# Moving three operand splits, holding a fourth weight tile, and two tables of numbers in a fused attention, MLP and MLP kernel

## The chip, the core and the metric

The kernel runs on one core of a Trainium2 chip. The metric is the device time of one execution in microseconds (us). TensorE (PE) does the matmuls, VectorE (DVE), ScalarE (ACT) and GpSimd (POOL) the elementwise work, SyncE (SP) issues most of the DMAs, and POOL issues those that add while they copy.

## The reference

Chunked attention with a few memory keys, then two dense MLPs over 3072 tokens; only the shapes and the two MLPs matter here.

```python
x = attention(q, k, v, mem_k, mem_v)         # (3072, 512) after the heads are joined
def moe(x, w_in, w_out):                     # w_in (512, 2048), w_out (2048, 512)
    h = x @ w_in
    g = max(h, 0) + log1p(exp(-abs(h)))
    return g @ w_out
def moe2(x, w_in, w_out, alpha):             # the same shapes
    h = x @ w_in
    g = max(h, 0) + alpha * min(h, 0)
    return g @ w_out
out = moe2(moe(x))
```

## The kernel before

**Products of split operands.** Each float32 operand of the MLPs is kept as a high part (a rounded copy) and a low part (the rest), and one product is three matmuls: high by high, high by low, low by high. `high` makes the first by an ACT cast, `low` the second by a DVE subtraction; `ready(n)` does both for one operand of the second MLP. The split tiles `g` have three rooms, so a split is made at most two or three operands ahead of its matmuls.

**First part: attention and the first MLP.** 96 steps, each a product into `ps_hh` and one into `ps_o` of 12 matmuls. Attention tiles, the conversion of both layers' weights from 64-bit words (`convert_a`, `convert_b` on DVE, tiles `word`) and sums of the second layer's weights (`wsum`, `wst` on POOL and ACT, written to `in_ops` and `out_ops` in DRAM) are set among the steps by a planner, the class `Plan`: each piece has an engine, a guessed duration and a due time, and the planner emits the piece that can start first, and of those the one due first. Its order is the order of the program on every engine, since the engines work in order. `when[i]` is the planned time of step `i`; line 806 sets the due times of the 32 conversions of the second layer.

**Second part: the second MLP.** Tokens go in three pairs of blocks of 512. Both matmuls of a pair use a seven-product scheme on two by two blocks (as Strassen's, in Winograd's form). In the first half of a pair, eight quads (`quad`, L553) each make seven products of six matmuls into four PSUM banks, combine them with the copies `c1`, `c5` (ACT, tiles `tc`) and the sums `u2` and `plus` (DVE), and apply the activation; `G[k, q]` (tiles `gb`) is the result. In the other half (`second`, L618) seven passes of eight units each (56 units of six matmuls) use `w_out` tiles of 1 MB, each for four units: tile `k` serves units `4k` to `4k + 3`. The operands of the first units, `G[1, 0]` to `G[1, 2]`, are made in the first quads, long before.

**DMAs of the second half.** `load_w_out` brings a tile. `SUMS` names after which unit POOL issues an in-place addition of 1 MB, `slots[k, half] += slots[e, half]`, which makes an operand of a later pass. `load_y` brings the first MLP's results for the next pair (tiles `yraw`, four loads for each `h`), `sum_y` and `split_y` (tiles `yt`, `xop`) prepare them on DVE and ACT; `prepare` says in which units. At the end `load_w_in` brings the next pair's first weights. SP issues its DMAs in one order, and a DMA that waits for a room holds those behind it. All large tiles (`w_out`, `w_in`, `xop`, `gb`) share sixteen rooms.

Of the kernel before, what the change touches and what calls it, by code (L numbers as in the profile page):

```python
# [44 lines left out]
NQ = NF // 2  # L45
# [89 lines left out]
def attention_mlp_mlp_kernel(ctx: ExitStack, tc, qk, v, w1, w2, consts, out):  # L135
# [363 lines left out]
    PASSES = ((S1, T1, 1), (A11, B11, 0), (S2, T2, 1), (S3, T3, 0), (S4, B22, 3), (A12, B21, 2), (A22, T4, 1))  # L499


    SUMS = {4: (0, 1, 3), 8: (1, 1, 3), 12: (0, 0, 1), 16: (1, 0, 1), 24: (0, 1, 2), 28: (1, 1, 2)}

    def load_w_out(n):

# [5 lines left out]
    def product(p, n, ka, kb, ps, first):  # L511
        w, x = w_in.pop((n, ka)), x_op[p, kb]
        k = 0
        for h in range(2):
            for a, c in ((0, 0), (0, 1), (1, 0)):
                pe.matmul(
                    ps, lhsT=w[:, a, h * P:(h + 1) * P], rhs=x[:, c, h, :],
                    start=first and k == 0, stop=k == 5, skip_group_check=not first,
                )
                k += 1  # L520
# [24 lines left out]
    def copy(ps, tag, bufs=1):  # L545
        t = tpool.tile([P, N2], F32, tag=tag, name="tc", bufs=bufs)
        act.copy(out=t, in_=ps)
        return t

    def plus(out, in0, in1, op=ALU.add):  # L550
        dve.tensor_tensor(out=out, in0=in0, in1=in1, op=op)

    def quad(p, q, between, ahead):  # L553


        n, f0, f1 = p * NQ + q, 2 * q, 2 * q + 1
        if q % 4 == 0:
            for k in range(4):
                room = (wpool if k else xpool).tile([P, 4, N2], F32, tag="w" if k else "x", name="gb")
                slots[k, q // 4] = room  # L560
                for e in range(4):
                    G[k, q + e] = room[:, e, :]
        banks = [("acc", ps_acc)] * 4 if q % 2 else [("pa", ps_a), ("h", ps_h)] * 2
        x1, x4, x3, x2 = (bank(space, tag) for tag, space in banks)
        product(p, n, A11, B11, x1, True)
        c1 = copy(x1, "tb")
        product(p, n, S1, T1, x4, True)
        c5 = copy(x4, "tl")
        product(p, n, S2, T2, x2, True)
        u2 = tpool.tile([P, N2], F32, tag="ta", name="u2", bufs=2)  # L570
        plus(u2, x2, c1)
        product(p, n, S3, T3, x3, True)
        plus(x3, x3, u2)
        plus(G[3, q], x3, c5)
        n3 = negative(G[3, q], f1)
        between()
        product(p, n, A12, B21, x1, False)
        n0 = halves_of(x1, G[0, q])
        product(p, n, S4, B22, x4, False)
        ahead()  # L580
        prelu(G[3, q], n3, G[3, q])
        plus(G[1, q], x4, u2)
        minus_prelu(n0, f0, G[0, q])
        n1 = negative(G[1, q], f0)
        product(p, n, A22, T4, x3, False)
        prelu(G[1, q], n1, G[1, q])
        dve.scalar_tensor_tensor(out=G[1, q], in0=G[1, q], scalar=-1.0, in1=G[0, q], op0=ALU.mult, op1=ALU.subtract)
        n2 = halves_of(x3, G[2, q])
        minus_prelu(n2, f1, G[2, q])
        if q < NQ - 2:  # L590
            load_w_in(n + 2)
        else:
            for k in range(3)[2 * q - 2 * NQ + 4:][:2]:
                load_w_out(14 * p + k)

    def turn(c, b, d):

# [15 lines left out]
    def ready(n):  # L613
        i, q = divmod(n, NQ)
        src = G[PASSES[i][2], q]
        g2[n] = low(src, high(src, n))

    def second(p, todo):  # L618

        ps_of, kept, c, later = {}, {}, {}, []  # L620
        spaces = {S1: (ps_acc, "acc"), A11: (ps_h, "h"), S2: (ps_a, "pa"), S3: (ps_acc, "acc"), S4: (ps_a, "pa"), A22: (ps_acc, "acc")}

        def temp(key, m, tag):
            kept[key, m] = tpool.tile([P, N2], F32, tag=tag, name="u2", bufs=1 if tag in ("tb", "tl") else 2)
            return kept[key, m]

        def result(d, b, m):
            if m == 0:
                c[d, b] = rpool.tile([P, 2, N2], F32, tag="raw", name="c")
            return c[d, b][:, m, :]  # L630

        def after(ka, ps):

            sub = ALU.subtract
            if ka == S1:
                return [lambda m=m: act.copy(out=temp("p5", m, ("tb", "tl")[m]), in_=ps[m]) for m in range(2)]
            if ka == A11:
                return [lambda m=m: act.copy(out=temp("p1", m, "word"), in_=ps[m]) for m in range(2)]
            if ka == S2:
                return [lambda m=m: plus(temp("u2", m, "ta"), ps[m], kept["p1", m], sub) for m in range(2)]  # L640
            if ka == S3:
                return ([lambda m=m: plus(temp("u3", m, "word"), ps[m], kept["u2", m]) for m in range(2)]
                        + [lambda m=m: plus(result(1, 1, m), kept["u3", m], kept["p5", m], sub) for m in range(2)]
                        + [lambda m=m: plus(kept["u2", m], kept["u2", m], kept["p5", m], sub) for m in range(2)])
            if ka == S4:
                return [lambda m=m: plus(result(0, 1, m), ps[m], kept["u2", m]) for m in range(2)]
            if ka == A12:
                return [lambda m=m: act.activation(out=result(0, 0, m), in_=ps[m], func=AF.Identity, scale=-1.0) for m in range(2)]
            return [lambda m=m: plus(result(1, 0, m), kept["u3", m], ps[m], sub) for m in range(2)]

        for n in range(7 * NQ):
            i, q = divmod(n, NQ)
            ka = PASSES[i][0]
            w = w_out[14 * p + n // 4][:, n % 4]
            if q == 0:
                ps = ps_of[ka] = [bank(*spaces[ka]) for _ in range(2)] if ka in spaces else ps_of[A11]
            g = g2.pop(n)
            for m in range(2):
                for k, (a, e) in enumerate(((0, 0), (0, 1), (1, 0))):
                    pe.matmul(  # L660
                        ps[m], lhsT=w[:, a, m * P:(m + 1) * P], rhs=g[:, e, :], start=ka in spaces and q == 0 and k == 0,
                        stop=q == NQ - 1 and k == 2, skip_group_check=ka not in spaces,
                    )
            if n % 4 == 3:
                w_out.pop(14 * p + n // 4)
                if n // 4 + 3 < 14:
                    load_w_out(14 * p + n // 4 + 3)
            if n in SUMS:
                half, k, e = SUMS[n]
                nc.gpsimd.dma_start(out=slots[k, half], in_=slots[e, half], accum_op=ALU.add)  # L670
            if 0 < n < 7 * NQ - 2:
                ready(n + 2)
            if q == NQ - 1:
                later = after(ka, ps)
                while i == 6 and later:
                    later.pop(0)()
            elif later:
                later.pop(0)()
            if q == 6 and i > 3:
                d, b = ((1, 1), (0, 1), (0, 0))[i - 4]  # L680
                turn(c.pop((d, b)), 2 * p + b, d)
            for piece in todo.get(n, ()):
                piece()
            if n == 7 * NQ - 8 or n == 7 * NQ - 4:
                load_w_in((p + 1) * NQ + (n == 7 * NQ - 4))
        return lambda: turn(c.pop((1, 0)), 2 * p, 1)

    def prepare(p):

        if p >= NPAIRS:  # L690
            return {}
        todo = {}
        for h in range(2):
            at = 2 + 25 * h
            todo[at] = [lambda h=h: load_y(p, h)]
            for k in range(3):
                todo[at + 7 + k] = [lambda h=h, k=k: sum_y(p, h, k)]
            for n, k in enumerate((B11, B21, B22, T1, T2, T3, T4)):
                todo[at + 10 + 2 * n] = [lambda h=h, k=k: split_y(p, h, k)]
            todo[at + 11] = [lambda h=h: sum_last(p, h)]  # L700
        return todo

    def pairs(between):
        for p in range(NPAIRS):
            for q in range(NQ):
                quad(p, q, between, (lambda: [ready(n) for n in range(3)]) if q == NQ - 1 else lambda: None)
                between = lambda: None
            between = second(p, prepare(p + 1))
        between()
# [9 lines left out]
    when = [ZERO + STEP * i for i in range(len(steps) + 1)]  # L719
# [83 lines left out]
    add(("raw2", 0), "", 5.0, 0, lambda: load_raw(1, halves[0]), [("raw", 2 * NF - 1)], ["raw"])  # L803
    for j in range(4 * NQ):
        q, e = divmod(j, 4)
        k, due = halves[j], when[20 + 60 * j // (4 * NQ)]
        add(("ca2", j), "DVE", 1.35, due, lambda j=j: convert_a(1, halves[j]), [("raw2", j)] + ([("cv2", j - 1)] if j else []), ["word"])
        add(("cv2", j), "DVE", 1.42, due, lambda j=j: convert_b(1, halves[j]), [("ca2", j)], [], ["raw"])
        if j + 1 < 4 * NQ:
# [124 lines left out]
```

## Time and profile before

| | us |
|---|---|
| median of three runs | 1166.56 (1164.11 to 1166.74) |
| the profiled execution, its own time | 1168.74 |
| its span, first to last instruction | 1166.9 |
| PE busy | 1119.8 (96%) |
| DVE busy | 734.2 (63%) |
| ACT busy | 573.9 (49%) |
| POOL busy | 183.1 (16%) |
| mean granted TensorE clock of the core | 0.982 |

A busy share says only how long an engine had an instruction. What the kernel loses stands in the gaps of PE, in what ended each gap, and in the stretches in which the granted clock is below 1.

### The profile page before, as it was taken

To read this page: it belongs to the slowest core of one execution; us is meant where nothing else is said; L and a number is where in the kernel's file an instruction comes from. 1 tells how busy PE (TensorE), PEld (TensorE's weight loads), DVE (VectorE), ACT (ScalarE), POOL (GpSimd) and SP (SyncE) were. 2 spreads that over 40 slices of the span, in tenths; PEclk is the share of its full clock that TensorE was granted. 3 is DMA by queue.
4 is the path that set the end of the run, shared out by engine and by line. 5 is a ranking of instruction groups with operands and counts; after the bars stand their busy time and mean duration, and the time that the engine had idled before them with its cause. 6 is when DMAs were issued, how large, how long until landed. Compare 5 with 4: busy or idle time off the path is not lost.

```text
span 1166.9 us, 15807 instructions
## 1 busy us (share of the span) xinstructions
PE 1119.8 (96%) x5760; PEld 924.2 (79%) x5760; DVE 734.2 (63%) x1486; ACT 573.9 (49%) x1068; POOL 183.1 (16%) x182
## 2 busy tenths in 40 slices
PE   6889999999999999999999999998999989999998
PEld 5767888877888888888888888787888778887776
DVE  5978878666656555665442266677566658566464
ACT  5854334455534544453343255654455546456433
POOL 0101222434333243333230000010000100000100
PEclk9988999999999999999999999999999999999999
DMA  8833564657645554554344074899356896647961
GB/s 307 268 98 120 159 150 144 170 181 209 204 140 190 178 174 129 192 165 158 129 142 162 3 286 163 274 225 400 117 228 222 238 293 257 220 165 288 304 164 67
DMA packets 76765, 224.12 MB, mean 192 GB/s; under 512 B 6160, under 2 KB 28688, under 8 KB 69008
## 3 DMA queue, kind: packets, MB, share of 16 engines
q1 hardware_dynamic: 71792, 200.05, 48.7%
q0 software_dynamic: 4896, 23.07, 10.4%
q8 instruction: 45, 0.74, 0.3%
q14 instruction: 32, 0.26, 0.1%
HBM read 158.08 MB, written 46.14 MB: 175 GB/s over the span
## 4 chain that ended last, share of the span: by engine, by line
PE 77%; DVE 7%; DMA 7%; issue 5%; ACT 2%; POOL 1%; SPq 0%; POOLq 0%; ACTq 0%; DVEq 0%
PE ps_q L61 35%; PE ps_o L61 18%; PE ps_hh L61 18%; DMA wout<-out_ops 3%; PE ps_s L61 3%; DVE word L61 2%; PE ps_x L61 2%; PE ps_t L61 1%; DMA in_ops<-wst 1%; DMA gb<-gb 1%; DVE g L61 1%; DVE gb L61 1%; DMA qk<-in_qk_dram 1%; ACT tp L61 1%; DVE s_sb L61 1%
## 5 line engine op out<-in xcount | busy, mean ns | idle before, releaser
L61 PE MATMUL ps_o<-g,wsplit 128*128 128x512 f32 x1152 | 283.0, 395 | 3.5 <-DVE g L61 2.7
L61 PE MATMUL ps_hh<-x,wsplit 128*128 128x512 f32 x1152 | 282.3, 396 | 2.3 <-DVE x L61 1.3
L61 PE MATMUL ps_q<-g,wout 128*128 128x512 f32 x1008 | 243.7, 401 | 15.8 <-DMA wout<-out_ops 6.5
L61 PEld LDWEIGHTS ps_hh<-x,wsplit 128*128 128x128 f32 x1152 | 216.8, 190 | 47.9 <-DVE x L61 2.0
L61 PEld LDWEIGHTS ps_o<-g,wsplit 128*128 128x128 f32 x1152 | 215.7, 189 | 49.3 <-DVE g L61 3.5
L61 PEld LDWEIGHTS ps_q<-g,wout 128*128 128x128 f32 x1008 | 193.1, 193 | 62.7 <-ACT g L61 9.1
L61 PE MATMUL ps_q<-xop,win 128*128 128x512 f32 x1008 | 229.7, 389 | 0.0
L61 PEld LDWEIGHTS ps_q<-xop,win 128*128 128x128 f32 x1008 | 189.0, 188 | 39.2
L61 DVE TENSOR_TENSOR g<-ta,g 128x512 fp32r<-128x512 f32 x96 | 76.1, 795 | 145.5 <-ACT g L61 145.4
L61 DVE TENSOR_TENSOR g<-gb,g 128x512 fp32r<-128x512 f32 x168 | 112.7, 688 | 84.3 <-ACT g L61 83.4
L61 ACT CAST g<-gb 128x512 fp32r<-128x512 f32 x168 | 100.3, 621 | 107.3 <-PE ps_q L61 80.2
L61 ACT ACTIVATE ta<-ps_hh 128x512 f32<-128x512 f32 x96 | 57.5, 599 | 188.9 <-PE ps_hh L61 186.5
L670 POOL DMA_DIRECT2D gb<-gb x18 | 15.7, 871 | 502.4 <-DVE g L61 476.9
L61 DVE SCALAR_TENSOR_TENSOR word<-raw,word 128x512 int32<-128x512 int32 x128 | 92.0, 719 | 3.8
L61 ACT ACTIVATE tp<-gb 128x512 f32<-128x512 f32 x48 | 30.4, 633 | 98.6 <-DVE gb L61 98.5
L219 POOL TENSOR_TENSOR wst<-wsum,wst 128x512 fp32r<-128x512 f32 x32 | 44.0, 1376 | 141.3 <-ACT wst L61 127.6
L61 PE MATMUL ps_s<-qk 128*128 128x96 f32 x384 | 55.7, 299 | 10.2 <-DMA qk<-in_qk_dram 6.9
L61 ACT CAST g<-ta 128x512 fp32r<-128x512 f32 x96 | 59.7, 622 | 10.1 <-PE ps_o L61 8.0
L61 PEld LDWEIGHTS ps_s<-qk 128*128 128x128 f32 x384 | 53.2, 212 | 13.8 <-DMA qk<-in_qk_dram 6.0
L61 DVE SCALAR_TENSOR_TENSOR gb<-gb,tp 128x512 f32<-128x512 f32 x48 | 33.2, 692 | 48.4 <-ACT tp L61 48.4
L61 DVE TENSOR_SCALAR word<-word 128x512 f32<-128x512 f32 (+1 forms) x128 | 58.7, 459 | 4.4
L61 ACT ACT_TABLE_LOAD x40 | 51.3, 1283 | 1.4 <-PEq L924 0.7
(67 smaller groups left out, 980.4 us busy)
## 6 DMA issues: line engine op xcount, KB each, us to landing
wout<-out_ops SPq DMA_DIRECT2D x42, 1024.0 KB, 10.3
raw<-in_w_dram SPq DMA_DIRECT2D x64, 512.0 KB, 3.7
win<-in_ops SPq DMA_DIRECT2D x24, 1024.0 KB, 8.0
qk<-in_qk_dram SPq DMA_DIRECT2D x24, 832.0 KB, 5.6
win<-in_ops SPq DMA_DIRECT2D x24, 768.0 KB, 7.5
gb<-gb POOLq DMA_DIRECT2D x18, 1024.0 KB, 12.0
out_ops<-wst SPq DMA_DIRECT2D x56, 256.0 KB, 3.0
in_ops<-wst SPq DMA_DIRECT2D x24, 512.0 KB, 3.4
```

The costliest lines, as they stand in the source:

```text
L61: i = getattr(self.engine, name)(*args, **kw)
L219: nc.gpsimd.tensor_tensor(out=t[:, 1, :n], in0=src, in1=t[:, 0, :n].bitcast(F32), op=ALU.subtract)
L670: nc.gpsimd.dma_start(out=slots[k, half], in_=slots[e, half], accum_op=ALU.add)
```

## The change

The three splits of a pair's first units, which stood together behind the last quad's product S4, are made one behind the copy `c1`, one behind `c5`, and one behind the sum into `G[3, q]`. The last two quads load four `w_out` tiles, not three, and the loop over the units loads the tile that is four ahead, not three. Four of the six entries of `SUMS` stand at other units. `prepare` starts one unit earlier. The conversions of the second layer's weights are due from step 24 on, over 64 steps, not from step 20 over 60.

```diff
-    SUMS = {4: (0, 1, 3), 8: (1, 1, 3), 12: (0, 0, 1), 16: (1, 0, 1), 24: (0, 1, 2), 28: (1, 1, 2)}
+    SUMS = {3: (0, 1, 3), 7: (1, 1, 3), 12: (0, 0, 1), 16: (1, 0, 1), 29: (0, 1, 2), 36: (1, 1, 2)}
...
         product(p, n, A11, B11, x1, True)
         c1 = copy(x1, "tb")
+        ahead(0)
         product(p, n, S1, T1, x4, True)
         c5 = copy(x4, "tl")
+        ahead(1)
...
         plus(G[3, q], x3, c5)
+        ahead(2)
         n3 = negative(G[3, q], f1)
...
         product(p, n, S4, B22, x4, False)
-        ahead()
...
-            for k in range(3)[2 * q - 2 * NQ + 4:][:2]:
-                load_w_out(14 * p + k)
+            for k in range(2):
+                load_w_out(14 * p + 2 * (q - NQ + 2) + k)
...
-                if n // 4 + 3 < 14:
-                    load_w_out(14 * p + n // 4 + 3)
+                if n // 4 + 4 < 14:
+                    load_w_out(14 * p + n // 4 + 4)
...
-            at = 2 + 25 * h
+            at = 1 + 25 * h
...
-                quad(p, q, between, (lambda: [ready(n) for n in range(3)]) if q == NQ - 1 else lambda: None)
+                quad(p, q, between, ready if q == NQ - 1 else lambda n: None)
...
-        k, due = halves[j], when[20 + 60 * j // (4 * NQ)]
+        k, due = halves[j], when[24 + 64 * j // (4 * NQ)]
```

What stands on the engines, by the built programs:

ACT in the last quad of the first pair, from its copies on. `tc` are `c1` and `c5`, the casts to `g` are the high parts, `tp` and `gb` are the activation's steps. Before:

```order
L61 COPY tc<-ps_q 128x512 x2
L61 ACTIVATE tp<-gb 128x512
L61 ACTIVATE tp<-tp,cst 128x512
L61 ACTIVATE tp<-ps_q 128x512
L61 ACTIVATE gb<-ps_q 128x512
L61 CAST g<-gb 128x512 x3
```

After:

```order
L61 COPY tc<-ps_q 128x512
L61 CAST g<-gb 128x512
L61 COPY tc<-ps_q 128x512
L61 CAST g<-gb 128x512 x2
L61 ACTIVATE tp<-gb 128x512
L61 ACTIVATE tp<-tp,cst 128x512
L61 ACTIVATE tp<-ps_q 128x512
L61 ACTIVATE gb<-ps_q 128x512
```

The three casts moved ahead of the four activations that they followed. DVE in the same quad; the rows `g<-gb,g` are the low parts. Before:

```order
L61 TENSOR_TENSOR u_6350<-ps_q,tc 128x512
L61 TENSOR_TENSOR ps_q<-ps_q,u_6350 128x512
L61 TENSOR_TENSOR gb<-ps_q,tc 128x512
L61 TENSOR_TENSOR g<-gb,g 128x512 x3
L61 SCALAR_TENSOR_TENSOR gb<-gb,tp 128x512
L61 TENSOR_TENSOR gb<-ps_q,u_6350 128x512
```

After:

```order
L61 TENSOR_TENSOR g<-gb,g 128x512 x2
L61 TENSOR_TENSOR u_6356<-ps_q,tc 128x512
L61 TENSOR_TENSOR ps_q<-ps_q,u_6356 128x512
L61 TENSOR_TENSOR gb<-ps_q,tc 128x512
L61 TENSOR_TENSOR g<-gb,g 128x512
L61 SCALAR_TENSOR_TENSOR gb<-gb,tp 128x512
L61 TENSOR_TENSOR gb<-ps_q,u_6356 128x512
```

Two of the three subtractions moved ahead of `u2`, the third stayed behind the sum into `G[3, q]`. SP in the first pair (the second pair reads alike), from the end of its quads to the loads for the next pair. Before:

```order
L494 DMA win<-in_ops 128x2x768
L509 DMA wout<-out_ops 128x2048 x7
L460 DMA yraw<-y_dram 128x512
L509 DMA wout<-out_ops 128x2048
L460 DMA yraw<-y_dram 128x512 x3
L509 DMA wout<-out_ops 128x2048 x6
L494 DMA win<-in_ops 128x2x1024
```

After:

```order
L494 DMA win<-in_ops 128x2x768
L509 DMA wout<-out_ops 128x2048 x8
L460 DMA yraw<-y_dram 128x512 x2
L509 DMA wout<-out_ops 128x2048
L460 DMA yraw<-y_dram 128x512
L509 DMA wout<-out_ops 128x2048
L460 DMA yraw<-y_dram 128x512
L509 DMA wout<-out_ops 128x2048 x4
```

The eighth tile (number 7) moved ahead of all four `yraw` loads, number 8 ahead of two of them and number 9 ahead of one. In the third pair, which has no `yraw` loads, SP reads as before. POOL's rows, its six additions of each pair among them, stand in the order of before.

## Rows read from the trace of the kernel before

**Rows 1.** Waits of PE: who was waited for, us in total, times, longest.

```profile
PE ps_q L61 <- DMA wout<-out_ops: 6.5, 2, 3.5
PE ps_q L61 <- ACT g L61: 6.2, 7, 1.3
PE ps_q L61 <- DVE g L61: 3.1, 7, 0.7
...
PE ps_s L61 <- ACT pt L61: 2.4, 3, 1.5
```

**Rows 2.** PE's timeline, second part: start, us, matmuls, idle ahead and its end.

```profile
670.34 70.88 PE L61 MATMUL ps_q<-xop,win 128*128 128x512 f32 x312
...
748.95 39.49 PE L61 MATMUL ps_q<-g,wout 128*128 128x512 f32 x173 [0.74 <-DVE g L61]
791.94 11.14 PE L61 MATMUL ps_q<-g,wout 128*128 128x512 f32 x42 [3.50 <-DMA wout<-out_ops]
...
913.93 41.10 PE L61 MATMUL ps_q<-g,wout 128*128 128x512 f32 x173 [0.74 <-DVE g L61]
```

**Rows 3.** Stretches: length, busy PE, PEld, DVE, ACT, POOL, clock, DMA share, GB/s.

```profile
200.00:660.00 460.00, 454.62 (x2557) 377.30 (x2557) 258.26 (x594) 206.37 (x339) 138.79 (x136) 1.00 0.51 162
236.00:244.00 8.00, 7.43 (x60) 6.63 (x61) 5.33 (x23) 2.47 (x7) 2.09 (x2) 0.79 0.61 174
792.00:796.00 4.00, 4.00 (x12) 3.20 (x13) 0.00 (x0) 0.00 (x0) 0.00 (x0) 0.65 1.02 430
914.00:918.00 4.00, 4.00 (x11) 3.13 (x12) 1.77 (x3) 0.62 (x1) 0.87 (x1) 0.57 0.66 133
958.00:964.00 6.00, 5.98 (x19) 4.77 (x20) 0.91 (x3) 0.62 (x1) 0.00 (x0) 0.72 1.01 427
1080.00:1086.00 6.00, 5.76 (x18) 4.59 (x19) 3.18 (x6) 1.76 (x3) 0.97 (x2) 0.72 1.02 374
```

**Rows 4.** ACT's timeline in the first pair's last quad.

```profile
734.24 1.08 ACT L61 COPY tc<-ps_q 128x512 f32<-128x512 f32 x2
...
739.37 0.72 ACT L61 ACTIVATE tp<-tp,cst 128x512 f32<-128x512 f32 x1
...
740.95 1.66 ACT L61 CAST g<-gb 128x512 fp32r<-128x512 f32 x3
```

**Rows 5.** DVE's timeline in the same quad and behind it.

```profile
735.88 0.69 DVE L61 TENSOR_TENSOR u<-ps_q,tc 128x512 f32<-128x512 f32 x1 [0.39 <-PE ps_q L61]
737.17 0.70 DVE L61 TENSOR_TENSOR ps_q<-ps_q,u 128x512 f32<-128x512 f32 x1 [0.60 <-PE ps_q L61]
...
741.60 1.90 DVE L61 TENSOR_TENSOR g<-gb,g 128x512 fp32r<-128x512 f32 x3 [2.93 <-ACT g L61]
743.42 0.68 DVE L61 SCALAR_TENSOR_TENSOR gb<-gb,tp 128x512 f32<-128x512 f32 x1
...
748.21 1.89 DVE L61 TENSOR_TENSOR g<-gb,g 128x512 fp32r<-128x512 f32 x3
```

**Rows 6.** SP's timeline of DMA issues, first pair.

```profile
722.21 18.00 SPq L509 DMA_DIRECT2D wout<-out_ops  x7
...
766.39 1.15 SPq L509 DMA_DIRECT2D wout<-out_ops  x1
769.10 5.36 SPq L460 DMA_DIRECT2D yraw<-y_dram  x3
774.55 14.24 SPq L509 DMA_DIRECT2D wout<-out_ops  x5
```

**Rows 7.** The DMA issued at 774.5: count, KB, us from issue to landing.

```profile
wout<-out_ops SPq DMA_DIRECT2D x1, 1024.0 KB, 17.3
```

**Rows 8.** The stretch of the six additions, columns as in rows 3.

```profile
750.00:788.00 38.00, 38.00 (x169) 31.49 (x168) 26.19 (x42) 22.00 (x39) 4.44 (x6) 1.00 1.01 221
```

**Rows 9.** POOL's timeline, first pair: the fifth of the six additions.

```profile
769.97 0.87 POOL L670 DMA_DIRECT2D gb<-gb  x1 [4.82 <-DVE g L61]
```

**Rows 10.** The chain that ended last, third pair, ahead of unit 28.

```profile
1101.15 15.33 DMA gb<-gb
```

## Prediction

> **What bounds the kernel now.** I began with the busy shares (PE 96%) and then asked what ends PE's gaps. The view of waits [rows 1] gives three causes in the second part: w_out tiles that have not landed (6.5 us, twice), and high and low parts of operands `g` (6.2 and 3.1 us, seven times each). PE's timeline [rows 2] says where. The eight quads run without a gap, 312 matmuls in 70.88 us, so a matmul has a slot of 0.227 us; then the first four units of the other half stutter, and at 791.94 PE waits for a tile. The view by stretches [rows 3] adds what no wait shows: behind such a gap the granted clock mostly falls, for some us, to its lower level (1.2 of 2.4 GHz). So the kernel is bound by PE, with losses at a few places:
>
> - Start of the units. From 670.34 to the second matmul of unit 3, at 748.95, lie 331 matmuls [rows 2], 75.2 us at 0.227; it took 78.6. The loss is 3.4 us, and the first part of rows 1's waits repeats it in each of three pairs. In the second pair the clock then stands at 0.57 for 4 us, in the third at 0.72 for 6 [rows 3]: 0.43 x 4 = 1.7 and 0.28 x 6 = 1.7 us. In the first pair it does not fall (1.00 from 750 on [rows 8]).
> - Tile 8. The 173 matmuls from 748.95 would end at 788.25; unit 32 starts at 791.94, 3.7 us late, and the clock takes 0.35 x 4 = 1.4 us more. The second pair has 3.0 (what is left of 6.5), 3.2 by position, and 1.7 of clock at 958.
> - Unit 28 of the third pair, behind an addition that took 15.33 us [rows 10].
> - First part, 200 to 660 us: 460 - 454.6 = 5.4 us of idle PE, and 0.21 x 8 = 1.7 us of clock at 236 [rows 3]: with the fill of the pipeline some 8 us.
>
> **The splits (moved).** Before, three casts (740.95, 1.66 us) and three subtractions (741.60, 1.90 us) stand on ACT and DVE in the middle of the last quad's activation [rows 4, 5]. ACT had finished what DVE's step at 743.42 needs by 740.09 (739.37 + 0.72): that step, and the whole chain to the low part of unit 3 (the first of three at 748.21), waits 3.3 us for the subtractions. In the new order the first two splits go into the idle time ahead. That isn't quite free: ACT has two copies from 734.24 (1.08 us) and now two casts with them (1.1), so the second high part is there at 736.4, its subtraction ends at 737.0, and `u2` starts there, not at 735.9. Behind it the sum at 737.17 had 0.6 us of slack on PE, so it becomes 0.7 later (the third subtraction then runs while ACT works). DVE's step thus starts at 740.8, 2.6 us earlier, and so does the chain to unit 3: its low part is there at 746.3. PE, with units 0 to 2 ready at once, wants it at 670.34 + 75.2 = 745.5. **2.65 us of the 3.4 are gained, 0.8 stay.** A gap of that size cost no clock where I see one (the first pair's larger one didn't), so the 1.7 us in pairs two and three go too.
>
> **Tiles and y loads (moved).** The first seven tiles leave SP from 722 on, in one burst [rows 6]: a tile goes as soon as a room is free, not at the unit where the code has it. Tile 7 then stands behind the first `yraw` load (766.39), and tile 8 behind the next three, which wait for rooms that DVE's work on `xop` gives back; it is issued only at 774.55 and takes 17.3 us [rows 6, 7]. What it waits for otherwise is tile 2's room, free since unit 11, near 761. In the new order tile 7 is in the burst, and tile 8 goes behind the second `yraw`, at 769.10 before; `prepare`, one unit earlier, takes 1.4 us off that and the start of the units 2.65. So it is issued near 765, and unit 32 wants it at 746.3 + 39.3 = 785.6. With its 17.3 us it lands at 782. That price lies high: tile 7's place in the queue is gone from ahead of it, though two loads and the additions still share the engines.
>
> A limit remains. From 750 on the DMA engines are full (share 1.01 over 38 us [rows 8]), so until 791.8 they moved what they could: six additions, four `yraw`, tiles 7 and 8. With tile 7 in the burst, tile 9 takes its place in that sum, and lands between 789 and 792.5; unit 36 wants it 24 matmuls after unit 32, at 791.0. I leave 0.7 us in each pair for it (bounds 0 and 1.5, and 1.4 more if the clock falls). Behind unit 23 the order of tiles is as before.
>
> First pair: 2.65 + 3.7 + 1.4 - 0.7 = 7.0 us. Second pair: 2.65 + 1.7 + 3.2 + 1.7 - 0.7 = 8.5 us.
>
> **The third pair.** It has no `yraw` loads, and its SP order is unchanged. Unit 28 waits for the fourth addition, which waits for the second, and that for the low part of unit 7; an addition takes 15 us there [rows 10]. This chain starts with the first operands, 2.65 us earlier. What PE gains beyond, the 1.7 us of clock, it waits at unit 28, and the clock falls there as before. Gain 2.65 us (bounds 1 and 8, worked out below).
>
> **`SUMS` (four entries moved).** Nothing. The fifth addition stands behind unit 24 in the code, yet POOL issued it at 769.97, when PE was 92 matmuls past 748.95, in unit 18; it had waited for a subtraction of DVE [rows 9]. POOL does little else in the second part, its order is unchanged, and its additions wait for the operands read before, which are the same ones. Units 29 and 36 don't hold it back either.
>
> **Due times of the conversions.** They start four steps later, when the first layer's conversions are nearly done, and lie a little further apart; the last ends some five steps later, under 80 to 86 of 96, where PE has no gap. The order of DVE, ACT, POOL and SP in the first part changes throughout, so each of the old gaps can go and new ones come. Bounds: all 8 us gained; two places like that at 236 (1.5 us of waiting [rows 1] and 1.7 of clock) lost, 6.4 us. I take 2 us of gain, nearer to nothing.
>
> **Sum.** 7.0 + 8.5 + 2.65 + 2 = 20.2 us. The profiled execution took 1168.7 us (span 1166.9), so 1148.5; the runs' median is 2.2 us below the profile, so 1146.4 for a median. I say 1147.
>
> **Rivals.**
> A. *The full DMA engines stay the bound in pairs one and two.* All that changes for tile 8 is then that tile 7 (2.4 us at the 430 GB/s of the stretch at 792 [rows 3]) is out of the way: it lands at 791.8 - 2.4 = 789.4, PE waits 3.8 us at unit 32, and the clock falls as before. Pair one gains 2.5 us, pair two some 3.3 to 4, with the rest 10.5 to 11: 1156. For it: share 1.01 [rows 8], and 17.3 us for 1 MB. Against: within those 41.8 us tile 8 was issued late, so two additions got ahead of it that now run beside it. [...]
> B. *The third pair's additions are not the bound.* The second one is issued some 4 us earlier (2.65, and unit 7 lay behind the slow clock). If the chain keeps up, unit 28's wait (the last of the seven in rows 1's first two kinds, 1.5 us, about 2 by position) and the clock's fall behind it, 1.7 as elsewhere, go as well as the 1.7 ahead: 8 us for the pair, and with a better first part 1141. Against: tiles and additions share the engines there, and starting additions earlier puts them beside more of the tiles.
> C. *Slower: the first part's new order.* ACT takes its casts of `wst` in order, and one that waits for a staging room holds attention's copies behind it; at 236 that cost 1.5 + 1.7 us. Seven such places more than before would outweigh 20 us and make the kernel slower by the bound. For it: conversions now run through to the last attention tiles. Against: they are less dense, and the whole stretch has five us of gaps today.
> D. *The splits move and nothing follows*, because unit 0 waits for a PSUM bank: it needs the one that the activation of A12's product empties, just ahead of the casts at 740.95 before [rows 4] and 0.7 us later after; only the unit's second half uses it, three matmuls after the start at 741.2, so this costs 0.1 us at most. Little speaks for it.
>
> **How the numbers follow.** Forecast 0.58 (1143 to 1151), A 0.2 (1152 to 1158), B 0.1 (1138 to 1143), a first part that loses 3 to 6 us with the rest as forecast 0.07 (1150 to 1156), C 0.04, D 0.01. The range 1139 to 1157 leaves out about 0.15. What a measurement can tell from no change is 0.3%, 3.5 us: 1163 and 1170. Faster 0.93; same 0.04 (A with a loss in the first part); slower 0.03.
>
> **What would show it.** Right: PE's gaps at the start of the units shrink to one below 1 us at unit 3, with no fall of the clock behind it; tile 8 leaves SP some 7 us earlier against PE's progress and the wait for w_out in units 32 to 36 is below 1.5 us a pair; the third pair still waits at unit 28, longer than before; POOL's additions keep their places between PE's units. Wrong: a w_out wait of 3 us or more (A), new waits of PE of more than 8 us in all between 200 and 660 (C), a chain on DVE that is late by more than 0.7 us at `u2`, or a gap between units 33 and 46, where DVE has a subtraction, a combination and y work in nearly every unit and no time to spare.

## The result and the profile after

The changed kernel took 1146.57 us (median of four runs, 1145.29 to 1147.35) against 1165.96 us of before in the same runs: a ratio of 0.9835, 95% interval 0.9818 to 0.9852. It is faster by 1.65%, 19.4 us; the prediction was 1147. The profiled execution took 1145.29 us, its span is 1143.4.

PE's waits in the second part, where [rows 1] had three kinds; w_out is gone from the list:

```profile
PE ps_q L61 <- ACT g L61: 3.1, 3, 2.2
PE ps_q L61 <- DVE g L61: 2.7, 7, 0.6
```

PE's timeline of the second part, answering [rows 2] (start, us, matmuls, idle ahead and what ended it; the rows left out have at most 0.23 us of idle time ahead of them):

```profile
665.12 70.88 PE L61 MATMUL ps_q<-xop,win 128*128 128x512 f32 x312
...
741.05 49.05 PE L61 MATMUL ps_q<-g,wout 128*128 128x512 f32 x215 [0.63 <-DVE g L61]
...
803.32 0.51 PE L61 MATMUL ps_q<-g,wout 128*128 128x512 f32 x1 [0.18 <-ACT g L61]
...
823.33 70.98 PE L61 MATMUL ps_q<-xop,win 128*128 128x512 f32 x312
...
899.37 49.09 PE L61 MATMUL ps_q<-g,wout 128*128 128x512 f32 x215 [0.59 <-DVE g L61]
...
962.28 0.50 PE L61 MATMUL ps_q<-g,wout 128*128 128x512 f32 x1 [0.74 <-ACT g L61]
...
982.29 70.98 PE L61 MATMUL ps_q<-xop,win 128*128 128x512 f32 x312
...
1058.32 29.06 PE L61 MATMUL ps_q<-g,wout 128*128 128x512 f32 x126 [0.63 <-DVE g L61]
1087.60 5.55 PE L61 MATMUL ps_q<-g,wout 128*128 128x512 f32 x23 [0.23 <-DVE g L61]
1095.38 0.50 PE L61 MATMUL ps_q<-g,wout 128*128 128x512 f32 x1 [2.22 <-ACT g L61]
1096.10 15.07 PE L61 MATMUL ps_q<-g,wout 128*128 128x512 f32 x65 [0.23 <-DVE g L61]
```

From 741.05 on, and from 899.37 on in the second pair, 215 matmuls run without a gap, where before they broke at unit 32. Two gaps are left in the first two pairs: below 1 us at unit 3, and one at unit 47 that the kernel before did not have. The third pair waits at units 24 and 28. Stretches, columns as in [rows 3], and the stretch of [rows 8]:

```profile
200.00:660.00 460.00, 458.50 (x2589) 381.33 (x2588) 258.70 (x599) 208.24 (x343) 139.11 (x136) 1.00 0.51 162
750.00:788.00 38.00, 38.00 (x169) 31.46 (x168) 29.17 (x47) 21.70 (x39) 3.48 (x4) 1.00 1.02 279
1095.00:1103.00 8.00, 7.40 (x31) 5.88 (x32) 4.53 (x8) 4.27 (x8) 0.87 (x1) 1.00 1.02 281
```

The first part's idle time fell from 5.4 to 1.5 us. The DMA engines are as full as before. Behind the longest gap the clock stays at 1.00. SP in the first pair, answering [rows 6]:

```profile
716.99 18.48 SPq L509 DMA_DIRECT2D wout<-out_ops  x8
756.74 2.28 SPq L460 DMA_DIRECT2D yraw<-y_dram  x2
759.11 1.19 SPq L509 DMA_DIRECT2D wout<-out_ops  x1
762.57 0.32 SPq L460 DMA_DIRECT2D yraw<-y_dram  x1
762.99 1.42 SPq L509 DMA_DIRECT2D wout<-out_ops  x1
```

POOL's fifth addition, answering [rows 9], 96.7 us behind the first quad's start (99.6 before):

```profile
761.84 0.87 POOL L672 DMA_DIRECT2D gb<-gb  x1 [4.19 <-DVE g L61]
```

DVE in the last quad, answering [rows 5]; two subtractions stand ahead of `u2` now, and the step into `G[3, q]` at 735.51 no longer waits for three:

```profile
731.17 0.69 DVE L61 TENSOR_TENSOR g<-gb,g 128x512 fp32r<-128x512 f32 x1 [0.29 <-ACT g L61]
731.78 0.68 DVE L61 TENSOR_TENSOR u<-ps_q,tc 128x512 f32<-128x512 f32 x1
...
735.51 0.69 DVE L61 SCALAR_TENSOR_TENSOR gb<-gb,tp 128x512 f32<-128x512 f32 x1 [0.92 <-ACT tp L61]
...
740.32 1.89 DVE L61 TENSOR_TENSOR g<-gb,g 128x512 fp32r<-128x512 f32 x3
```

The chain that ended last, ahead of unit 28 of the third pair, answering [rows 10]:

```profile
1079.17 15.43 DMA gb<-gb
```

**Where the time went.** The starts of the three quad stretches and of the last seven transposes (1137.76 after, 1161.20 before) cut an execution into four pieces. One execution is a weak witness, since the order of instructions doesn't change from run to run but the falls of the clock do. The profiled executions of the kernels below are used too, each for the pieces in which its order is that of before or that of the change. Means, with range and number of executions:

| piece | order of before | order of the change | gained | forecast |
|---|---|---|---|---|
| first part, to the first quad | 670.1 (668.7 to 672.2; 4) | 665.0 (661.8 to 666.5; 10) | 5.2 | 2 |
| first pair | 165.6 (164.9 to 166.6; 3) | 158.6 (158.2 to 158.8; 4) | 7.0 | 7.0 |
| second pair | 165.5 (164.4 to 166.3; 3) | 158.9 (158.5 to 159.3; 4) | 6.6 | 8.5 |
| third pair | 158.8 (157.5 to 160.0; 4) | 156.5 (155.5 to 157.4; 6) | 2.3 | 2.65 |

Their sum, 21.1 us from few executions, stands beside 19.4 by the medians.

### The profile page after: what moved, and what is told of

Read it like the earlier page. It is cut to its first block, busy times and chain, and to the rows that moved or that the text cites. A ratio compares the mean times of both kernels' runs of the same rounds, so it can differ in the third digit from the quotient of the medians.

```text
span 1143.4 us, 15784 instructions
## 1 busy us (share of the span) xinstructions
PE 1110.9 (97%) x5760; PEld 919.2 (80%) x5760; DVE 732.1 (64%) x1486; ACT 573.4 (50%) x1068; POOL 183.5 (16%) x182
## 3 DMA queue, kind: packets, MB, share of 16 engines
q0 software_dynamic: 4896, 23.07, 10.5%
## 4 chain that ended last, share of the span: by engine, by line
PE 83%; DMA 6%; DVE 5%; ACT 3%; POOL 1%; issue 1%; SPq 0%; ACTq 0%; DVEq 0%; POOLq 0%
PE ps_q L61 33%; PE ps_o L61 21%; PE ps_hh L61 21%; PE ps_s L61 3%; PE ps_x L61 2%; PE ps_t L61 2%; DMA out_dram<-o_sb 2%; DVE gb L61 2%; ACT tp L61 1%; DMA gb<-gb 1%; DMA in_ops<-wst 1%; DMA qk<-in_qk_dram 1%; DMA out_ops<-wst 1%; DVE g L61 1%; POOL wst L219 1%
## 5 line engine op out<-in xcount | busy, mean ns | idle before, releaser
L61 PE MATMUL ps_q<-g,wout 128*128 128x512 f32 x1008 | 235.2, 392 | 6.0 <-ACT g L61 3.1
L61 PEld LDWEIGHTS ps_q<-g,wout 128*128 128x128 f32 x1008 | 187.7, 188 | 49.8 <-DVE g L61 6.3
L61 DVE TENSOR_SCALAR word<-word 128x512 f32<-128x512 f32 (+1 forms) x128 | 62.9, 491 | 4.4
L219 POOL TENSOR_TENSOR wst<-word,wst 128x512 fp32r<-128x512 f32 (+1 forms) x32 | 36.6, 1144 | 118.4 <-ACT wst L61 118.4
```

The source lines that it names most:

```text
L61: i = getattr(self.engine, name)(*args, **kw)
L219: nc.gpsimd.tensor_tensor(out=t[:, 1, :n], in0=src, in1=t[:, 0, :n].bitcast(F32), op=ALU.subtract)
```

## The experiments

Ratios are to the kernel before, run beside each kernel on the same chip, with the 95% interval. A difference in us that stands behind a ratio is worked out from the ratio; a difference of two medians can lie up to 1.5 us off it.

**The splits alone.** The kernel before, with only this:

```diff
         c1 = copy(x1, "tb")
+        ahead(0)
...
         c5 = copy(x4, "tl")
+        ahead(1)
...
         plus(G[3, q], x3, c5)
+        ahead(2)
...
-        ahead()
```

> The kernel before, with the splits of units 0 to 2 moved and nothing else. Theory (the units' start and tile 8 are separate losses, and tile 8 is late because of its place in SP's queue): each pair gains the 2.65 us at unit 3, pair two 1.7 us of clock behind it, and the third pair what it gained in the whole change, 4.2 us; tile 8's wait stays as it was: about 2.65 + 4.35 + 4.2 = 11 us less than before, at least 8. Rival (the full DMA engines bound unit 32): what PE gains at unit 3 of pairs one and two it waits for at tile 8 instead, w_out waits of 9 us there in place of 6.5 to 7 in all, and only the third pair's 2.65 to 4.2 us are left: 3 to 5 us less than before.

Measured: 1157.79 us, 0.9925 (0.9903 to 0.9947), 8.7 us less. Unit 3's gap shrank as in the whole change. But the two waits for tile 8 grew, to 4.31 and 3.54 us, from 6.5 in all [rows 1] to 7.9. Tile 8 in the first pair, its issue, who waited for it, and its time to land:

```profile
L509 SPq DMA_DIRECT2D wout<-out_ops x1: 665/665/665, 770.3 to 770.3; - x1
...
  PE ps_q L61: 4.3, 1
...
DMA to landing us min/median/max: 18.1/18.1/18.1
```

It left 2.6 us earlier against the first quad (101.6 us behind it, 104.2 before) and landed 1.8 us earlier (119.7 and 121.5). Against the means of before the pairs are 1.3, 3.1 and 1.9 us shorter, and the first part 1.4. The size is at the lower end of the theory's (at least 8), and the pieces of this one execution add up to 7.7; in the first pair the rival's mechanism is at work.

**Tiles and y work alone.** The kernel before with `k + 4` tiles held and `at = 1 + 25 * h`.

> The kernel before, with four w_out tiles held and the y work one unit earlier; splits, additions and due times as before. Theory (order of issue): tile 8 leaves SP some 8 us earlier, its wait and the clock's fall behind it go in pairs one and two (3.7 + 1.4 and 3.2 + 1.7 us), the 3.4 us at the start of the units stay in all three: 10 us less than before, no wait for w_out above 1 us. Rival (full DMA engines): only tile 7's 2.4 us are saved in each of the two pairs, and the clock still falls: about 5 us less, with w_out waits of 1.3 and 0.8 us left.

Measured: 1157.42 us, 0.9931 (0.9915 to 0.9947), 8 us less, and no wait for w_out. Pairs one and two took 160.9 and 161.6 us, 4.7 and 3.8 less than the means of before. That lies between theory and rival in time, but the rival's left-over waits aren't there.

**Four tiles, and the y work's unit.** Two kernels take one of these back from the changed kernel. Three tiles held:

```diff
-                if n // 4 + 4 < 14:
-                    load_w_out(14 * p + n // 4 + 4)
+                if n // 4 + 3 < 14:
+                    load_w_out(14 * p + n // 4 + 3)
```

> The changed kernel with three w_out tiles held, as before; all else of the change kept. SP then sends tile 7 where the changed kernel sends tile 8, and tile 8 where it sends tile 9 (762.99 there, 20.7 us to its landing at 783.7; unit 32 wants it at 780.4). Theory (place in the queue decides): unit 32 waits 1 to 3.3 us in pairs one and two and the clock may fall behind it, 1.5 more: 3 to 8 us more than the changed kernel. Rival (the y work's earlier unit did it alone, the fourth tile nothing): within 1 us of the changed kernel.

The y work at its old unit (`at = 2 + 25 * h`):

> The changed kernel with the y work at its unit of before; all else of the change kept. SP then has one y load ahead of tile 8 and three more ahead of tile 9. Theory: tile 8 lands in time; tile 9 leaves some 101.5 us behind the first quad's start, as tile 8 did where the splits alone were moved, takes 18 to 20.7 us and is wanted 120.7 us behind that start: waits of 0 to 1.5 us in pairs one and two, 1.5 of clock with each at most: 0 to 6 us more than the changed kernel. Rival (four tiles did it alone): within 1 us of the changed kernel.

Measured: three tiles 1152.26 us, 0.9876 (0.9853 to 0.9899), 4 to 6 us slower than the change, as the theory had it. The old unit 1144.94 us, 0.9814 (0.9792 to 0.9837): not slower than the change, as the rival had it, with no difference clear of the noise; its first two pairs took 158.9 and 159.0 us, against means of 158.6 and 158.9 in the change. PE's timeline with three tiles, at unit 32:

```profile
783.97 11.17 PE L61 MATMUL ps_q<-g,wout 128*128 128x512 f32 x42 [3.44 <-DMA wout<-out_ops]
```

Tile 8 of that kernel, issue and landing:

```profile
L509 SPq DMA_DIRECT2D wout<-out_ops x1: 1040/1040/1040, 763.0 to 763.0; - x1
...
DMA to landing us min/median/max: 20.9/20.9/20.9
```

Tile 9 of the changed kernel, in the same place of SP's queue:

```profile
L509 SPq DMA_DIRECT2D wout<-out_ops x1: 1421/1421/1421, 763.0 to 763.0; - x1
...
DMA to landing us min/median/max: 20.7/20.7/20.7
```

The second tile behind the burst, by issue and landing in us behind the first quad's start:

| kernel | which tile | issued | landed |
|---|---|---|---|
| before | 8 | 104.2 | 121.5 |
| splits alone | 8 | 101.6 | 119.7 |
| change, old y unit | 9 | 101.6 | 119.4 |
| change, three tiles | 8 | 97.9 | 118.8 |
| change | 9 | 97.9 | 118.6 |

Leaving 6.3 us earlier brings 2.9 us, of which 1.8 came with the splits alone, which start the additions earlier as well. Between the change and the change with the old unit, where only the y work differs, 3.7 us bring 0.8. The place in time hardly counts, since the engines are full; what counts is that with a tile more in the burst the tile that lands at 119 is number 9, which unit 36 wants at 120.7, and not number 8, which unit 32 wants at 115.2 (741.05 - 665.12, 173 matmuls of 0.227 on, and 24 more).

**Due times alone.** The kernel before with `when[24 + 64 * j // (4 * NQ)]`.

> The kernel before, with the new due times of the conversions alone. Theory: no other part of the change reaches the first part, so this gives all of what the first part gained with the change, 5.2 us up to the first quad, of which 6.4 us lie behind 100 us and 1.2 us are lost ahead of it; pairs as before. Rival: the first part's gain needs nothing of the order but came from this execution's clock at the start (0.87 to 0.88 in the first 100 us); then this kernel gains below 2 us, as I forecast.

Measured: 1160.96 us, 0.9962 (0.9948 to 0.9976), 4.4 us less; the first quad starts at 666.50. PE's gaps in the first part behind 200 us, all four:

```profile
220.94 2.02 PE L61 MATMUL ps_s<-qk 128*128 128x96 f32 x16 [0.58 <-DVE x L61]
232.30 1.13 PE L61 MATMUL ps_s<-qk 128*128 128x96 f32 x8 [0.23 <-ACT pt L61]
...
627.12 0.50 PE L61 MATMUL ps_o<-g,wsplit 128*128 128x512 f32 x1 [0.27 <-ACT g L61]
628.50 2.79 PE L61 MATMUL ps_o<-g,wsplit 128*128 128x512 f32 x11 [0.89 <-DVE g L61]
```

In the order of before, in four executions, there are seven to nine, nearly all at the same places, among them 0.5 to 1.4 and 0.9 us at 286 and 1.1 at 305. They have none near 627: the gap there is new with the later due times, and the changed kernel has it too (0.77 us at 627.13). The 1.2 us that the change seemed to lose ahead of 100 us are no loss: an execution in the order of before shows them as well (the 36 matmuls that start at 90.55 in the change start at 90.39 with the splits alone).

**`SUMS` alone.**

> The kernel before, with the four additions moved to other units in the code and nothing else. Theory: POOL's order and what each addition waits for are the same, so the time is that of before within 0.1%, and unit 28 of the third pair waits as it did. Rival (the third pair's 4.2 us in place of 2.65 came from the additions of units 3 and 7): 1.5 us less than before, with the wait at unit 28 shorter by that.

Measured: 1165.29 us, 0.9993 (0.9980 to 1.0006): nothing. By the built programs it has the instructions of before, in their order and with the same waits, on all five engines, so this edit alone could not bring the rival about. The same program, and yet its second and third pair were 1.9 and 1.7 us shorter in the profiled execution than in that of before: two falls of the clock that did not come.

**The third pair's additions.** The changed kernel without the first four of them (`if n in SUMS and (p < 2 or n > 16)`), so that pair's output lacks what they add:

> The changed kernel without the first four additions of the third pair; that pair's results are wrong by what they add, all other work is done. Theory (the chain of additions is what unit 28 waits for there): the wait of 2.2 us at unit 28 and the 0.2 ahead of it go and nothing comes in their place: 2 to 3 us less than the changed kernel, in some runs 1.7 us more where the clock would have fallen. Rival (the w_out tiles are next and come as late): 0 to 1 us less, with PE waiting for w_out in units 28 to 36.

And with tile 8 there held back: POOL writes a column of its room from what the second addition wrote, so that its load has to wait for that addition.

```diff
+    def load_w_out(n, after=None):
...
+        if after is not None:
+            nc.gpsimd.tensor_copy(out=t[:, 0, 0, 0:1], in_=after[:, 0, 0:1])
...
+                    load_w_out(14 * p + n // 4 + 4, slots[1, 1] if p == 2 and n == 19 else None)
```

> The changed kernel, with w_out tile 8 of the third pair (and so all tiles behind it on SP) held back until the second addition has landed. Theory (additions and tiles share the DMA engines, and the tiles slow the chain of additions): the first two additions land in 8 to 11 us in place of 12.7 and 15.9, the wait at unit 28 goes or falls below 0.5 us, tile 8 still lands ahead of unit 32: 1.5 to 3 us less than the changed kernel. Rival (an addition's own pace sets its 15 us): additions as long as before, unit 28 waits as before and tile 8 comes late: 0 to 5 us more.

Measured: without additions 1141.32 us, 0.9778 (0.9755 to 0.9801); third pair 151.6 us, 4.9 less than the mean of the change (expected were 2 to 3, and 1.7 more where the clock would have fallen), and no wait in units 24 to 36:

```profile
1060.00 49.03 PE L61 MATMUL ps_q<-g,wout 128*128 128x512 f32 x215 [0.63 <-DVE g L61]
```

With tile 8 held 1142.31 us, 0.9787 (0.9765 to 0.9808); third pair 153.1 us, 3.4 less than that mean, and unit 28's wait is 0.66 us:

```profile
1056.44 34.06 PE L61 MATMUL ps_q<-g,wout 128*128 128x512 f32 x149 [0.63 <-DVE g L61]
1091.17 0.51 PE L61 MATMUL ps_q<-g,wout 128*128 128x512 f32 x1 [0.66 <-ACT g L61]
1091.89 15.03 PE L61 MATMUL ps_q<-g,wout 128*128 128x512 f32 x65 [0.22 <-DVE g L61]
```

So the additions are the third pair's bound, and tiles that nobody wants yet slow them. But the second addition takes 14.1 us (15.9 in the change), not 8 to 11, and the edit did less than it was meant to do. By the built program tile 9 moved up ahead of the held tile 8: SP's order in the third pair is 0 to 7, 9, 8, 10 to 13. SP issued nine of the fourteen tiles before the hold, and only these five behind it:

```profile
1075.64 2.81 SPq L511 DMA_DIRECT2D wout<-out_ops  x5
```

The ninth, tile 9, was issued at 1051.4 and landed 20.0 us later, so it shared the engines with the first two additions (issued at 1056.68 and 1060.90). The last experiment below, which holds tile 9 as well, shows what they take without it.

**The change once more, and unit 47.** Four kernels, run together. The changed kernel unaltered:

> The changed kernel once more, unaltered, as the base for the other three. Theory (the same order of instructions gives losses that differ from execution to execution, because the clock falls behind some gaps and not behind others): a median of 1145 to 1149 us, the first quad's start anywhere from 661.5 to 666.5, and at unit 28 of the third pair the clock falls or does not. Rival (the profiled execution's picture is the kernel's own): first quad at 665 within 0.5, no fall behind unit 28, 155.5 us in the third pair.

The changed kernel with unit 47's operands in another room:

```diff
-        g = gpool.tile([P, 2, N2], F32R, tag="g", name="g") if n % 3 < 2 else staging("g")
+        g = gpool.tile([P, 2, N2], F32R, tag="g", name="g") if n % 3 < 2 or n == 47 else staging("g")
```

> The changed kernel, with the operands of unit 47 in a room of the pool of operands in place of the staging pool's, which the output's store still reads. Theory (the store's 9.6 us hold that cast): the wait at unit 47, 0.4 to 1.3 us in pairs one and two, falls to 0.3 or less, since unit 45 frees the room some 1.4 us ahead: 0.5 to 2 us less than the changed kernel. Rival (that room is no sooner free than the store's, or DVE is what is late there): 0 to 1 us more.

With tile 8 held as well:

> Both together: tile 8 of the third pair held until the second addition has landed, and unit 47's room. Theory: the two gains add, as they lie in different pairs: 2.4 us in the third, 0.5 to 2 in the others, 3 to 4.5 us less than the changed kernel. Rival (they don't add, or the hold's gain was one run's luck): below 2 us.

With tile 9 held too, until the fourth addition has landed:

> The same, with tile 9 and those behind it held in the third pair until the fourth addition has landed. Theory (what is left of the wait at unit 28, 0.9 us, is the fourth addition beside tiles 8 to 13): that addition, 14.8 us with tile 8 alone held, takes 10 to 12, and the wait goes: 0.5 to 1 us less again. Rival (tile 9, issued some 12 us ahead of unit 36, comes late beside the last two additions): PE waits 1 to 3 us for w_out at unit 36, and this is slower than with tile 8 alone held.

Measured: 1146.36 us, 0.9839 (0.9821 to 0.9857), for the change; 1146.88, 0.9840 (0.9819 to 0.9860), with unit 47's room; 1140.75, 0.9798 (0.9777 to 0.9819), with tile 8 held as well (4.8 us less than the change, where 3 to 4.5 were expected); 1143.25, 0.9814 (0.9796 to 0.9832), with tile 9 too.

The change once more shows the theory of chance: the same program, a shorter wait at unit 28, and now the clock falls (65 matmuls in 16.65 us, 15.07 in the execution shown above). PE's timeline:

```profile
1095.64 0.50 PE L61 MATMUL ps_q<-g,wout 128*128 128x512 f32 x1 [1.79 <-ACT g L61]
1096.37 16.65 PE L61 MATMUL ps_q<-g,wout 128*128 128x512 f32 x65 [0.23 <-DVE g L61]
```

The same stretch, columns as in [rows 3], the clock 0.79 where it was 1.00:

```profile
1095.00:1103.00 8.00, 7.13 (x23) 5.49 (x24) 3.37 (x6) 3.39 (x6) 0.87 (x1) 0.79 1.02 283
```

Unit 47: in the changed kernel ACT's cast waits for the output's store, which takes 9.6 us beside tiles and `win`; with the other room it doesn't. ACT's timeline there, in the changed kernel:

```profile
802.64 1.14 ACT L61 CAST g<-gb 128x512 fp32r<-128x512 f32 x2 [3.28 <-DMA out_dram<-o_sb]
```

And with the other room, where the casts' waits end with PE's and DVE's work:

```profile
800.81 0.62 ACT L61 CAST g<-gb 128x512 fp32r<-128x512 f32 x1 [1.58 <-PE ps_q L61]
802.17 0.62 ACT L61 CAST g<-gb 128x512 fp32r<-128x512 f32 x1 [0.74 <-DVE g L61]
```

In all three kernels with that room the first pair takes 157.4 us and the second 157.5 to 157.7, 1.1 and 1.3 us less than the means of the change. The runs' medians don't show these 2.4 us, with intervals of 2 us to each side: the cause of the wait is shown, its worth in the whole time is not. Holding tile 9 took the rest of unit 28's wait and gave it back: PE waited 0.92 us for w_out at unit 36, and the third pair took 153.0 us as with tile 8 alone. The rival was right there; the fourth addition was hardly shortened (issued at 1072.85, it released POOL at 1087.27, 14.4 us later). The built program says why: tiles 10 and 11 moved up ahead of the held tile 9, and with tile 8 they ran beside that addition, SP's order being 0 to 8, 10, 11, 9, 12, 13.

The first additions, though, had the engines nearly to themselves here, since tile 9 no longer ran beside them: the first landed in 9.9 us and the second, issued at 1061.73, in 10.5:

```profile
L674 POOL DMA_DIRECT2D gb<-gb x1: 869/869/869, 1061.7 to 1061.7; - x1
...
DMA to landing us min/median/max: 10.5/10.5/10.5
```

That is the 8 to 11 us which the theory had for tile 8's hold: its size was right for the order that was meant, in this one execution.

With tile 8 held the kernel is faster than the changed one too, with unit 47's room (0.9798) or without (0.9787). The intervals only just part from the change's (0.9821 to 0.9857 in the same runs), but the third pair takes 152.9 and 153.1 us, against 155.5 to 157.4 in six executions of the change's order.

## Why the prediction was right, point by point

**The whole.** 1147 said, 1146.57 measured. Two terms were off, the first part by +3.2 and the second pair by -1.9, and largely cancelled. That the total came within half a us is therefore luck in part. The terms of the first and third pair were met, that of the first by two smaller errors that cancel (0.7 us left for tile 9 that didn't come, 1.1 us at unit 47 that did).

**The splits: right.** The forecast had 2.65 us gained and 0.8 left. By the timelines the loss up to unit 3 fell from 3.4 us to 741.05 - 665.12 - 75.2 = 0.7. `u2` started at 731.78, right behind the second subtraction, and DVE's next step at 735.51, as the chain was drawn. No fall of the clock followed. Alone, though, the first pair kept 1.3 us of it: without the tile's edit PE waits for part of it at unit 32.

**Tile 8: the numbers right, the reason half wrong.** Forecast: issued near 765, landing at 782, in us behind the first quad 94.7 and 111.7. Measured: 94.0 and 110.3 (759.11 + 16.3). That 17.3 us was near the measured 16.3 is luck: a tile behind the burst took from 11.2 us (tile 7 before) to 20.9 from issue to landing, by what ran beside it. But the step that counted an earlier issue as an earlier landing failed: six us of issue bring three of landing, and the y work's earlier unit, credited with 1.4 us, is worth nothing that can be measured. The sentence that held is the one on the limit: until then the engines moved what they could, and tile 9 takes tile 8's place in that sum, as tile 8 takes that of tile 7 (107.3 before). Tile 9's landing was put at 118.7 to 122.2 and is 118.6, ahead of unit 36, so the 0.7 us left for it didn't come in either pair.

**Rival A: right on the full engines, wrong on the landing.** It took from the stretch only tile 7's 2.4 us and had tile 8 land 119.1 us behind the first quad. Tile 8 landed at 110.3, and PE didn't wait. What failed is the count of places: with tile 7 in the burst, tile 8 is itself the next one in the queue, and a place there isn't 2.4 us, for tiles 8 and 9 land 8.3 us apart (775.4 and 783.7) beside the additions. The 118.8 with three tiles is no test of the rival, though it is near its 119.1: there tile 7 still stands behind the burst. That the additions and the loads share the engines agrees with the Trainium skill ("DMA: Bandwidth & Descriptors", section "Issuing engines are not separate DMA queues"): DMAs started by different engines run on the same sixteen DMA engines and interleave. In one stretch of 8 us, with tile 8 held and unit 47's room, POOL's queue had 92% of the sixteen engines and SP's 11%.

**Second pair: mis-sized.** 8.5 said, 6.6 measured. 1.3 us are unit 47's wait, which was not foreseen: with the tile's wait gone, the store and its room are what is late next. (The warning looked at units 33 to 46, and at DVE.) That wait takes 1.1 us in the first pair too, where the 0.7 us that tile 9 didn't take cover most of it. Most of the rest is probably the clock: the forecast gave back two falls of 1.7 us as if they came in every run, and over three executions of the old order the pair takes 0.9 us less than in the one that was read.

**Third pair: right, with a wrong picture of the clock.** 2.65 said, 2.3 measured over executions, 4.2 in the one profiled. The fall behind unit 28 was put down as certain; it came in six of ten executions that wait there. The chain of additions as the bound is shown by taking it away, which rules out rival B, and the wait grew from 1.29 to 2.22 us, as said.

**`SUMS`: right**, 0.9993. **First part: mis-sized**, 2 said and 5.2 measured. Its bound of 8 was in the text; the choice "nearer to nothing" had no row behind it. The order decides here: executions of one order show nearly the same gaps. Why the new order has fewer was not traced further. Rivals C and D did not come.

## What to carry to other kernels

Where the DMA engines are full, don't count a transfer as earlier because it is issued earlier: count what stands ahead of it, and move whole transfers out of the full stretch into one with room (here 725 to 735 us, where the engines' share was 0.84). A transfer that nobody wants yet can be held back by a write to its room that reads the result of the one that is wanted; that gave a further 0.4 to 0.5% here, 3.4 to 3.6 us of it in the third pair. Look in the built program at what then moves up: here the next tile took the place of the held one. Before a removed wait is booked as gain, look for what is late next in the same units, on every engine and pool of rooms, and take a fall of the clock as a chance, not as a part of the gap.

## What the runs showed of the hardware

- **Falls of the clock are not fixed by the wait.** At unit 28 of the third pair ten executions waited 1.25 to 2.51 us. Behind five of them 65 matmuls took 16.6 to 16.7 us, behind a sixth 66 took 16.9, and behind four 65 took 15.0 to 15.1; the longest wait (2.51) had no fall, the shortest with one is 1.28. A fall there costs some 1.6 us.
- **The first 100 us differ from run to run**, in one order of instructions: the first quad starts between 661.8 and 666.5, and the granted clock over these 100 us was 0.95 in the execution of 661.8 (0.88 in that of 665.1).
- **In-place additions fill the DMA engines at half the bytes.** In the third pair with unit 47's room and tile 8 held, additions had nearly all of 1064 to 1072 us (the share of their queue, 92%; tile 9 had the rest), and 237 GB/s were moved at a share of 1.04; without the additions the tiles moved 418 GB/s at 1.01. The stretch with additions:

```profile
1064.00:1072.00 8.00, 8.00 (x37) 6.63 (x36) 3.90 (x7) 4.34 (x9) 0.87 (x1) 1.00 1.04 237
```

The stretch without them:

```profile
1064.00:1072.00 8.00, 8.00 (x37) 6.63 (x36) 3.90 (x7) 4.38 (x8) 0.00 (x0) 1.00 1.01 418
```
